# Two staging tiles, a separate mask matmul and a three-piece weight load in a recurrent attention kernel

## The chip, the cores and the metric

One core of a Trainium2 chip runs the whole program. The metric is the device time of one execution in microseconds (us). The kernel before took 2313.74 us (median of three runs, 2310.14 to 2330.06); its profiled execution took 2317.11 us, of which 2315.3 us lie between the first and the last instruction (the span).

## The reference

Two branches over the same input x (2048 rows of 1024, bf16) are mixed row by row with a gate. Branch B is a feed-forward net. Branch A is attention with a memory that is carried from segment to segment: 64 segments of 32 rows, each seeing 8 memory rows in front, 32 heads of 128.

```python
for s in range(n_seg):
    h = concatenate([mem, x[:, s*seg:(s+1)*seg, :]])     # 8 + 32 rows
    q, k, v = h @ Wq, h @ Wk, h @ Wv                     # 32 heads of 128 each
    p = softmax(where(mask, q @ k.T * scale, -1e9))
    o = (p @ v) @ Wo
    mem = o[:, :8]; outs.append(o[:, 8:])
a = concatenate(outs)
b = (gelu(x @ w_gate) * (x @ w_up)) @ w_down
g = sigmoid((x * gate_w).sum(-1)); out = g * a + (1 - g) * b
```

Segment s cannot start its projections before segment s-1 has given its 8 memory rows. The four attention weights are 32 MB in bf16 together, more than the core's on-chip memory holds.

## The kernel before

**Stages.** Up to about 1650 us of the span the program runs the 64 segments; after that come one pass over rows that were put aside and the feed-forward branch. The change touches the segments, and at the end of them two copies into `rb`.

**Rows of a segment.** TensorE takes 32 columns as its left side: 24 rows of the segment and the 8 memory rows (`hT0`, `hT1`, used in turn by segments). The other 8 rows of each segment need no memory for their own projections; they are projected four segments at a time from `hR` in the "fills" (`fill`, L844), and their results go out to the scratches `qk_scr` and `v_scr` and come back as `qkr` and `vB`.

**Heads and weights.** Heads come in two halves u = 0, 1. Each of Wq, Wk, Wv and Wo is cut into 8 pieces per half; a piece is 128 rows by 2048 columns, 512 KB or 4 KB per partition. Pieces with an index in `PAIRS` (two of k, two of q, five of v, five of o) share one slot between the two halves, so 14 of 64 pieces, 7 MB, are read again in every segment; the others stay. A slot is read again as soon as the last matmul on its old piece has run (`spent`). Some neighbouring slots are read by one DMA ("twins", `load_two`): k 0 and 1, q 0 and 1, v 0 and 1, v 2 and 3, o 4 and 5; v 4, o 0, o 1 and o 6 come alone. Wo is not laid out in the order that a piece needs, so a piece of it is written to `wo_scr` in segments 1 to 10 (`keep`) and from then on is read from there.

**Order.** All engines run lists in program order. The order comes from `walk` (the sequence of the 64 piece steps of a segment) and from hooks that `plan(s)` hangs on steps with `on(m, r, n, ...)`: m is the matrix, r = 0 the first half used in the segment and r = 1 the second, n the step. A segment's steps are: k r0 0-3, q r0 0-1, then o r1 4-7 of the segment before, q r0 2-3, v r0 0-3, k r0 4-7, q r0 4-7, v r0 4-7, then k r1, q r1, o r0, v r1 and o r1 0-3. `ua` and `ub` are the halves that a segment uses first and second. All weight loads, the load of the next `hT`, one load of `qkr` and the store of `oRc` are issued by SP, one after the other, and move through one DMA queue in that order; GpSimd (POOL) issues the loads of `vB` and of the other `qkr`, the stores of the fills and the store `a_scr` of a segment's output.

**One half of attention.** ACT copies k out of its PSUM bank into a staging tile (`evac`, L664), TensorE turns it (`turn`, L681), DVE copies it into `kT` (L667), POOL adds the 8 other rows from `qkr` (`put_rest`, L883); the same for q. `scores(u)` issues on TensorE the mask (one matmul of `mS` against the identity, 320 columns, L697) and 32 small score matmuls (L703) into bank SS, then the softmax on DVE and ACT up to `tAB` (L709 to L723). `attend(u)` (L732, L740) multiplies with `vA` and `vB`; `rest_o` (L757) puts 8 rows aside in `oRc`. After o r1, `fold` (L818, L819) adds two halves of the output through `part` into `a_bf`, and `next_mem` (L828, L831) turns the memory rows into the next `hT`.

**Who shares bytes with whom.** `hT0`, `vB` and `hT1` lie in a row, and `part` is two tiles over hT0+vB and vB+hT1. The staging tile of k of the second half ("p", `pS`) covers `oRc` and `a_bf`. The staging tile "o" covers `oT`, which is also `vA`: the second fill of a segment goes through it (`fill_evac`, `fill_put`, L876, store L879). Nearly every segment has a fill, two of four have a second one (`FILL`); the second is carried into the next segment.

Of the kernel before, what the change touches and what calls it, by code (L numbers as in the profile page):

```python
# [210 lines left out]
def bass_gated_mix__memory_aug_recurrent_mem_tr__geglu_ffn__prompt_kernel(  # L211
# [34 lines left out]
    with ExitStack() as es:  # L246
# [17 lines left out]
        wo_scr = nc.dram_tensor("wo_scr", [16, 128, 2048], BF16)  # L264

# [22 lines left out]
        hT0 = al("hT0", [128, KC, 32])  # L288
        vB = al("vB", [128, 2, 128])
        hT1 = al("hT1", [128, KC, 32])  # L290
        assert vB.off == hT0.off + 512 and hT1.off == vB.off + 512
        hT = (hT0, hT1)
        part = tuple(al(f"part{n}", [128, 256], FP32, at=o) for n, o in enumerate((hT0.off, vB.off)))
        qkr = al("qkr", [128, 3, 128])
        oRc = al("oRc", [128, NB, 32])
# [8 lines left out]
        assert a_bf.off == oRc.off + 512  # L304
        stage = {n: al(n + "S", [128, 512], at=t.off) for n, t in (("k", kT), ("q", qT), ("o", oT), ("p", oRc))}
# [69 lines left out]
        wo_at = lambda k: 8 * k[1] + k[2]  # L375

        def load_piece(t, k, lane):
            if k in kept:
                op("sp", lambda e: e.dma_start(t[:, :], wo_scr[wo_at(k)]), rd=[("D", "wo", k)], wr=[t.r()], lane=lane)
            else:  # L380
                op("sp", lambda e: e.dma_start(dst(t, k), src(k)), wr=[t.r()], lane=lane)

        def keep(k):
            t = slots[home[k]]
            op("sp", lambda e: e.dma_start(wo_scr[wo_at(k)], t[:, :]), rd=[t.r()], wr=[("D", "wo", k)], lane="wo")
            kept.add(k)
# [21 lines left out]
        twin = {("k", 1): 0, ("q", 1): 0, ("v", 1): 0, ("v", 3): 2, ("o", 5): 4}  # L408
        both = {}
        for (m, i1), i0 in twin.items():  # L410
            n0, n1 = home[m, 0, i0], home[m, 0, i1]
            assert i1 == i0 + 1 and n1 == n0 + 1 and slots[n1].off == slots[n0].off + PIECE
            both[m, i1] = ((wall, n0 - nkqv) if m == "o" else (sl, n0))
        held = set()

        def due(n):
            if done[n] < len(uses[n]) and uses[n][done[n]] != uses[n][done[n] - 1]:
                nk = uses[n][done[n]]
                return (nk, nk in moved and done[n] == len(uses[n]) - 1)
            return (None, False)  # L420

        def joined(k0, k1):
            return all(k is not None and not mv for k, mv in (k0, k1)) and (k0[0][0] != "o" or (k0[0] in kept and k1[0] in kept))

        def load_two(k0, t, x):
            m, u, i = k0
            k1 = (m, u, i + 1)
            reg = ("S", t.off + x * PIECE, t.off + (x + 2) * PIECE)
            if m == "o":
                a = wo_at(k0)  # L430
                op("sp", lambda e: e.dma_start(t[:, x:x + 2, :], wo_scr[a:a + 2].rearrange("y p c -> p y c")),
                   rd=[("D", "wo", k0), ("D", "wo", k1)], wr=[reg], lane=f"sl{home[k0]}")
            else:
                W = {"q": A_Wq, "k": A_Wk, "v": A_Wv}[m]
                v = W[i * 128:(i + 2) * 128, 16 * u:16 * u + 16, :].rearrange("(y p) h e -> p y (h e)", y=2)
                op("sp", lambda e: e.dma_start(t[:, x:x + 2, :], v), wr=[reg], lane=f"sl{home[k0]}")

        def reload(n, d):
            nk, mv = d
            if nk is None:  # L440
                return
            if mv:
                load_piece(moved[nk], nk, f"sl{n}")
            else:
                fetch(n)

        def spent(k):
            n = home[k]
            assert uses[n][done[n]] == k
            done[n] += 1  # L450
            m, u, i = k
            d = due(n)
            if (m, i + 1) in twin and d[0] is not None:
                held.add((m, i))
                both[m, i] = d
                return
            if (m, i) in twin and (m, i - 1) in held:
                held.remove((m, i - 1))
                d0 = both.pop((m, i - 1))
                if joined(d0, d):  # L460
                    load_two(d0[0], *both[m, i])
                    return
                reload(n - 1, d0)
            reload(n, d)
# [201 lines left out]
        def dve_copy(o, i, rd, wr):  # L666
            op("dve", lambda e: e.tensor_copy(o, i), rd=rd, wr=wr)  # L667
# [26 lines left out]
        def scores(u):  # L694

            def f(e):
                e.matmul(PB[SS][:, 0:320].rearrange("p (a c) -> p a c", a=4), lhsT=ident[:, :],  # L697
                         rhs=mS[:, :].unsqueeze(1).to_broadcast([128, 4, 80]), start=True, stop=False, skip_group_check=True)
                for n, c in ((32, 0), (8, 40)):
                    for j in range(4):  # L700
                        for g in range(4):
                            x = 8 * (4 * j + g)
                            ins = e.matmul(PB[SS][32 * g:32 * g + n, j * 80 + c:j * 80 + c + LQ],  # L703
                                           lhsT=qT[:, j, g, :] if n == 32 else qkr[:, 2 * u, x:x + 8],
                                           rhs=kT[:, j, g, :], start=False, stop=True, skip_group_check=True)
                return ins
            op("pe", f, rd=[qT.r(), qkr.r(256 * u, 256 * u + 128), kT.r(), ident.r(), mS.r()], wr=[BK(SS)])
# [14 lines left out]
            for c in (0, 256):  # L722
                op("dve", lambda e, c=c: e.transpose(tAB[:, c:c + 256], pAB[:, c:c + 256]), rd=[pAB.r(c, c + 256)], wr=[tAB.r(c, c + 256)], after=[fin])  # L723
# [91 lines left out]
        def fold(s, b):  # L815
            lo, hi = slice(64 * b, 64 * b + 64), slice(64 - 64 * b, 128 - 64 * b)
            pt, cs = part[s % 2], slice(256 * b, 256 * b + 256)
            op("dve", lambda e: e.tensor_copy(pt[lo, :], PB[XO][hi, cs]), rd=[BK(XO)], wr=[pt.r()])  # L818
            op("dve", lambda e: e.tensor_tensor(out=a_bf[lo, :], in0=PB[XO][lo, cs], in1=pt[lo, :], op=ALU.add),  # L819
# [83 lines left out]
        def plan(s):  # L903
# [29 lines left out]
            if not last:  # L933
# [10 lines left out]
            if s > 0:  # L944
                on("v", 0, 7, lambda: scores(ua))
# [3 lines left out]
            if s == 0:  # L949
                on("k", 1, 1, lambda: scores(ua))  # L950
# [7 lines left out]
            on(*(("q", 1, 1) if s else ("o", 0, 0)), lambda: evac(bank_of["k", 1], stage["p" if s else "k"], "act"))  # L958
            if s > 0:
                on("o", 0, 0, lambda: attend(ua, ((0, "dve"),), TT))  # L960
                on("o", 0, 0, lambda: evac(bank_of["q", 1], stage["q"], "act"))
                on("o", 0, 0, lambda: trans(kT, "p", A0))
                on("o", 0, 0, lambda: put_rest())
                on("o", 0, 0, lambda: take(((1, "act"), (2, "act"))))
                on("o", 0, 2, lambda: trans(qT, "q", SS))
# [3 lines left out]
            else:  # L969
# [4 lines left out]
                on("o", 0, 6, lambda: scores(ub))  # L974
# [38 lines left out]
        fold(NSEG - 1, 1)  # L1013
# [4 lines left out]
        for b in range(NBK):  # L1018
            rb = rbs[b % 2]
            for hf in range(2):  # L1020
# [9 lines left out]
                cp[("act", "dve")[hf]](rb[0:RB, hf * 512:hf * 512 + 512], PB[bk][0:RB, :], [BK(bk)], [rb.r(hf * 512, hf * 512 + 512)])  # L1030
# [143 lines left out]
```

## Time and profile before

| what | value |
|---|---|
| median of the runs shown (lowest to highest) | 2313.74 us (2310.14 to 2330.06) |
| profiled execution, and its span | 2317.11 us, 2315.3 us |
| TensorE matmul busy, weight load busy | 2130.5 us (92%), 1060.6 us (46%) |
| VectorE (DVE), ScalarE (ACT), GpSimd (POOL) busy | 1028.5 us, 543.2 us, 433.0 us |
| bytes moved by DMA | 638.35 MB |
| granted TensorE clock, mean | 0.986 |

In the lines of the profile, L774 is line 774 of the kernel before, and a tile name left of `<-` is what is written. "Idle before" is the time that the engine stood still ahead of an instruction, with what ended it. A timeline line gives start, duration, engine, line, operation and shapes; several instructions in a row are merged (x36). A DMA line is the issue, not the transfer; when a transfer has landed is read from its semaphore.

### The profile page before, as it was taken

The numbers are of one execution on the slowest core, as the hardware profiler recorded it, in microseconds if no ns is written. First come the engines' busy times: TensorE is split into PE (matmuls) and PEld (weight loads), VectorE is DVE, ScalarE is ACT, GpSimd is POOL, SyncE is SP. The second block draws the span as 40 slices with busy tenths as digits, with TensorE's granted clock in tenths as the row PEclk, the third lists the DMA queues.
The fourth block names the chain that finished last, engine by engine and source line by source line (L and its number), as shares of the span: only waits on it lengthen the run. The fifth ranks groups of instructions, "written<-read, shape, count | busy, mean of one in ns | idle before, by whom it ended". The sixth has DMA issues, their size and how long they took to land.

```text
span 2315.3 us, 74604 instructions
## 1 busy us (share of the span) xinstructions
PE 2130.5 (92%) x33852; PEld 1060.6 (46%) x33852; DVE 1028.5 (44%) x2440; ACT 543.2 (23%) x1111; POOL 433.0 (19%) x821
## 2 busy tenths in 40 slices
PE   4488999999999999999999999998899999999999
PEld 2244444444444444444454445444464444444444
DVE  3344444444444444444444444444315346163462
ACT  1122222222222222222222222222113123032130
POOL 4422222222222222222222222221100000000000
PEclk9799999999999999999999999999999999999999
DMA  9999999899898999989999899998964450803520
GB/s 373 353 306 333 333 338 348 305 337 333 314 336 319 328 340 324 345 323 334 347 327 349 310 335 345 320 331 319 340 201 159 137 163 10 285 25 117 178 88 19
DMA packets 251964, 638.35 MB, mean 276 GB/s; under 512 B 23256, under 2 KB 92120, under 8 KB 251648
## 3 DMA queue, kind: packets, MB, share of 16 engines
q1 hardware_dynamic: 227824, 596.59, 72.3%
q0 software_dynamic: 13888, 26.31, 3.8%
q10 hardware_dynamic: 9936, 10.69, 1.4%
q8 instruction: 266, 4.36, 0.7%
q14 instruction: 50, 0.41, 0.1%
HBM read 596.85 MB, written 36.63 MB: 274 GB/s over the span
## 4 chain that ended last, share of the span: by engine, by line
PE 66%; DMA 22%; DVE 4%; issue 4%; ACT 3%; POOL 1%; ACTq 0%; POOLq 0%; SPq 0%
PE pb L774 19%; PE pb L1075 15%; DMA sl<-in_A_Wv_dram 7%; PE pb L1129 5%; PE pb L807 5%; PE pb L844 5%; DMA qk_scr<-oS 4%; PE pb L790 4%; PE pb L681 3%; PE pb L1026 3%; PE pb L854 2%; DMA qkr<-qk_scr 2%; PE pb L1110 2%; DMA wall<-wo_scr 1%; DMA xr_scr<-xr 1%
## 5 line engine op out<-in xcount | busy, mean ns | idle before, releaser
L774 PE MATMUL pb<-sl,hT 128*32 128x512 bf16 x12288 | 771.9, 382 | 27.0 <-issue 19.4
L774 PEld LDWEIGHTS pb<-sl,hT 128*32 128x32 bf16 x12288 | 348.7, 97 | 310.5 <-issue 37.6
L844 PE MATMUL pb<-sl,hR 128*32 128x512 bf16 x3072 | 221.3, 390 | 2.4 <-issue 1.8
L1075 PE MATMUL pb<-xT,wg 128*128 128x512 bf16 x896 | 211.7, 379 | 0.7
L1075 PE MATMUL pb<-xT,wu 128*128 128x512 bf16 x896 | 211.7, 379 | 0.0
L807 PE MATMUL pb<-wall,oT 128*32 128x256 bf16 x4056 | 148.7, 274 | 17.8 <-DMA wall<-in_A_Wo_dram 7.0
L757 POOL COPY oRc<-oT 128x128 bf16<-128x128 bf16 x128 | 96.3, 752 | 361.7 <-DVE oT L667 360.2
L790 PE MATMUL pb<-wall,oT 128*32 128x512 bf16 x2048 | 153.2, 391 | 9.5 <-issue 6.2
L818 DVE COPY part<-pb 64x256 f32<-64x256 f32 x128 | 54.0, 422 | 235.3 <-PE pb L807 234.3
L664 ACT ACTIVATE kS<-pb 128x512 bf16<-128x512 f32 x127 | 75.8, 597 | 344.2 <-PE pb L774 322.4
L1129 PE MATMUL pb<-wd,GT 128*128 128x512 bf16 x672 | 146.3, 379 | 1.3 <-DMA wd<-in_B_w_down_dram 1.3
L711 ACT ACTIVATE E<-pb 128x320 bf16<-128x320 f32 x128 | 56.0, 438 | 371.6 <-DVE pb L710 371.6
L1083 ACT ACTIVATE s<-pb 128x512 f32<-128x512 f32 x112 | 66.8, 596 | 311.7 <-PE pb L1075 311.7
L1075 PEld LDWEIGHTS pb<-xT,wg 128*128 128x128 bf16 x896 | 87.2, 98 | 107.9 <-DVE GT L1091 3.7
L1075 PEld LDWEIGHTS pb<-xT,wu 128*128 128x128 bf16 x896 | 87.7, 98 | 105.7
L1084 DVE SCALAR_TENSOR_TENSOR tp<-s,pb 128x512 f32<-128x512 f32 x112 | 76.9, 687 | 124.2 <-ACT s L1083 124.0
L807 PEld LDWEIGHTS pb<-wall,oT 128*32 128x32 bf16 x4056 | 100.3, 96 | 67.6 <-ACT oT L664 26.1
L667 DVE CAST oT<-pb 128x160 bf16<-128x160 f32 x256 | 76.4, 320 | 115.2 <-PE pb L740 115.2
L667 DVE COPY kT<-pb 128x512 bf16<-128x512 bf16 x128 | 54.4, 425 | 158.1 <-PE pb L681 157.7
L664 ACT ACTIVATE vA<-pb 128x512 bf16<-128x512 f32 x128 | 76.2, 596 | 199.1 <-PE pb L774 151.7
L883 POOL COPY kT<-qkr 128x128 bf16<-128x128 bf16 x128 | 37.3, 292 | 431.2 <-DVE kT L667 272.5
L1088 DVE SCALAR_TENSOR_TENSOR tp<-tp,pb 128x512 f32<-128x512 f32 x112 | 77.0, 687 | 78.5 <-ACT tp L1087 78.5
(93 smaller groups left out, 2283.1 us busy)
## 6 DMA issues: line engine op xcount, KB each, us to landing
sl<-in_A_Wv_dram SPq DMA_DIRECT2D x128, 1024.0 KB, 11.2
wall<-wo_scr SPq DMA_DIRECT2D x175, 512.0 KB, 6.3
sl<-in_A_Wk_dram SPq DMA_DIRECT2D x64, 1024.0 KB, 5.8
sl<-in_A_Wq_dram SPq DMA_DIRECT2D x64, 1024.0 KB, 9.3
wall<-wo_scr SPq DMA_DIRECT2D x55, 1024.0 KB, 8.4
wd<-in_B_w_down_dram SPq DMA_DIRECT2D x42, 1024.0 KB, 5.6
sl<-in_A_Wv_dram SPq DMA_DIRECT2D x75, 512.0 KB, 11.6
wall<-in_A_Wo_dram SPq DMA_DIRECT2D x41, 512.0 KB, 7.7
```

The source lines that it names most:

```text
L664: op("act", lambda e: e.activation(o, i, ACTF.Copy), rd=rd, wr=wr)
L667: op("dve", lambda e: e.tensor_copy(o, i), rd=rd, wr=wr)
L681: ins = e.transpose(PBV[bank][:, j * 128:(j + 1) * 128], st[:, j * 128:(j + 1) * 128], ident[:, :])
L757: op("pool", lambda e: e.tensor_copy(oRc[:, :, 16 * u:16 * u + 16].rearrange("p c x -> p x c"), oT[:, :, :, 32:40].rearrange("p g j c -> p ...
L774: ins = e.matmul(PB[bk][32 * g:32 * g + 32, :], lhsT=h[:, i, :], rhs=w[:, g * 512:(g + 1) * 512], start=(n == 0), stop=(n == 7))
L790: ins = e.matmul(PB[XO][32 * g:32 * g + 32, :], lhsT=oT[:, j, x, 0:32], rhs=wall[:, na:nb + 1:nb - na, c:c + 256], start=(n == 0 and hp == 0),
L807: ins = e.matmul(PB[XO][32 * g:32 * g + 32, 256 * b:256 * b + 256], lhsT=oT[:, j, x, 0:32], rhs=w[:, c:c + 256], start=False, stop=(n % 4 ...
L844: ins = e.matmul(PB[b][32 * g:32 * g + 32, :], lhsT=h[:, k[2], :], rhs=w[:, g * 512:(g + 1) * 512], start=(n == 0), stop=(n == 7))
L1075: ins = e.matmul(PB[bk][:, 0:FB], lhsT=w[:, kc, cc:cc + 128], rhs=xT[:, :, :, kc, :].rearrange("p t i c -> p (t i) c"), start=(kc == 0), s ...
L1084: op("dve", lambda e, hg=hg, t=t: e.scalar_tensor_tensor(out=t[:, :], in0=s1[:, :], scalar=1.0, in1=hg, op0=ALU.add, op1=ALU.mult), rd=[BK ...
L1088: op("dve", lambda e, hu=hu, t=t: e.scalar_tensor_tensor(out=t[:, :], in0=t[:, :], scalar=1.0, in1=hu, op0=ALU.add, op1=ALU.mult), rd=[BK( ...
L1129: ins = e.matmul(PB[bank[2 * k + hf]][:, :], lhsT=GT[:, j, tb * 128:(tb + 1) * 128], rhs=w[:, jj, hf * 512:(hf + 1) * 512], start=(j == 0) ...
```

## The change

Line numbers of the new kernel differ by a few from those above; it keeps every computation.

1. Small tiles: the row is now `hT0`, `oRc`, `hT1`; `vB` has bytes of its own. The staging tiles 0 and 1 cover hT0+oRc and oRc+hT1 and replace "p" (k of the second half now goes through tile `ub`, the `hT` of the next segment) and "o" for the second fill (tile `ua`). `part` is one tile over `qT`. `a_bf` is no longer covered by a staging tile.
2. Moved because of that: the load of the next `hT` from k r0 4 to o r0 0, behind the turn of k; `load_v` of the next segment from q r0 2 to o r1 2 of the segment before; the copy out of the second fill's bank from q r0 2 to k r0 0, and its turn and store from v r0 3 to q r0 2.
3. The mask matmul is an operation of its own, right behind the turn of q (hooks v r0 5 and o r0 2); the second turn of q uses bank A1 in place of SS.
4. Pieces o 4, 5 and 6 lie in a scratch `wg_scr` as rows of 3 x 4 KB and are read by one DMA of 1.5 MB once all three slots are free.
5. Two copies at the end (`rb`) name the last `fold` as something to wait for.

```diff
+        wg_scr = nc.dram_tensor("wg_scr", [2, 128, 3, 2048], BF16)
...
         hT0 = al("hT0", [128, KC, 32])
+        oRc = al("oRc", [128, NB, 32])
+        hT1 = al("hT1", [128, KC, 32])
...
+        qkr = al("qkr", [128, 3, 128])
         vB = al("vB", [128, 2, 128])
-        part = tuple(al(f"part{n}", [128, 256], FP32, at=o) for n, o in enumerate((hT0.off, vB.off)))
...
+        part = al("part", [128, 256], FP32, at=qT.off)
+        stage = {n: al(f"{n}S", [128, 512], at=t.off) for n, t in (("k", kT), ("q", qT), ("o", oT), (0, hT0), (1, oRc))}
...
-        wo_at = lambda k: 8 * k[1] + k[2]
+        wo_at = lambda k: wg_scr[k[1], :, k[2] - 4, :] if 4 <= k[2] < 4 + 3 else wo_scr[8 * k[1] + k[2]]
...
+        GROUPS = {("k", 0): 2, ("q", 0): 2, ("v", 0): 2, ("v", 2): 2, ("o", 4): 3}
...
+                op("sp", lambda e: e.dma_start(t[:, x:x + n, :], wg_scr[u]), rd=[("D", "wo", (m, u, i + y)) for y in range(n)],
+                   wr=[reg], lane=f"sl{h}")
...
+        def mask():
+            op("pe", lambda e: e.matmul(PB[SS][:, 0:320].rearrange("p (a c) -> p a c", a=4), lhsT=ident[:, :],
+                                        rhs=mS[:, :].unsqueeze(1).to_broadcast([128, 4, 80]), start=True, stop=False,
+                                        skip_group_check=True), rd=[ident.r(), mS.r()], wr=[BK(SS)])
...
-            if not last:
+            if not last and s == 0:
                 on("k", 0, 4, lambda: load_h(s + 1))
...
             if s > 0:
+                on("v", 0, 5, mask)
                 on("v", 0, 7, lambda: scores(ua))
...
-            on(*(("q", 1, 1) if s else ("o", 0, 0)), lambda: evac(bank_of["k", 1], stage["p" if s else "k"], "act"))
+            on(*(("q", 1, 1) if s else ("o", 0, 0)), lambda: evac(bank_of["k", 1], stage[ub if s else "k"], "act"))
...
-                on("o", 0, 0, lambda: trans(kT, "p", A0))
+                on("o", 0, 0, lambda: trans(kT, ub, A0))
+                if not last:
+                    on("o", 0, 0, lambda: load_h(s + 1))
...
-                on("o", 0, 2, lambda: trans(qT, "q", SS))
+                on("o", 0, 2, lambda: trans(qT, "q", A1))
+                on("o", 0, 2, mask)
...
             if two:
-                on("q", 0, 2, lambda: fill_evac(*fl[1], B0, "o"), **nx)
+                on("k", 0, 0, lambda: fill_evac(*fl[1], B0, ua), **nx)
             on("q", 0, 2, lambda: fold(s, 1), **nx)
-            on("q", 0, 2, lambda: load_v(s + 1), **nx)
+            if two:
+                on("q", 0, 2, lambda: fill_put(*fl[1], ua, SS), **nx)
+            on("o", 1, 2, lambda: load_v(s + 1))
             on("v", 0, 3, lambda: next_mem(s, 1), **nx)
-            if two:
-                on("v", 0, 3, lambda: fill_put(*fl[1], "o", SS), **nx)
```

More of the change, by code (lines that the diff above doesn't have):

```diff
@@ L406, in first @@
                 fetch(n)
[L408 to L414, printed above, removed]
+        GROUPS = {("k", 0): 2, ("q", 0): 2, ("v", 0): 2, ("v", 2): 2, ("o", 4): 3}
+        lead = {(m, i + x): (m, i) for (m, i), n in GROUPS.items() for x in range(n)}
+        for (m, i), n in GROUPS.items():
+            assert all(home[m, 0, i + x] == home[m, 0, i] + x for x in range(n))
+        held = {}
         def due(n):
@@ L418, in due, with load_group, reload @@
                 nk = uses[n][done[n]]
[L419 to L425, printed above, removed]
+                return nk, nk in moved and done[n] == len(uses[n]) - 1
+            return None, False
+        def load_group(k0, n):
             m, u, i = k0
[L427 to L428 removed]
+            h = home[k0]
+            t, x = (wall, h - nkqv) if m == "o" else (sl, h)
+            reg = ("S", slots[h].off, slots[h].off + n * PIECE)
             if m == "o":
[L430 to L432 removed]
+                op("sp", lambda e: e.dma_start(t[:, x:x + n, :], wg_scr[u]), rd=[("D", "wo", (m, u, i + y)) for y in range(n)],
+                   wr=[reg], lane=f"sl{h}")
             else:
                 W = {"q": A_Wq, "k": A_Wk, "v": A_Wv}[m]
[L435 to L445, printed above, removed]
+                v = W[i * 128:(i + n) * 128, 16 * u:16 * u + 16, :].rearrange("(y p) h e -> p y (h e)", y=n)
+                op("sp", lambda e: e.dma_start(t[:, x:x + n, :], v), wr=[reg], lane=f"sl{h}")
+        def reload(n, nk, mv):
+            if nk is not None:
+                if mv:
+                    load_piece(moved[nk], nk, f"sl{n}")
+                else:
+                    fetch(n)
         def spent(k):
@@ L450, in spent @@
             done[n] += 1
[L451 to L455, printed above, removed]
-                return
[L457 to L464, printed above, removed]
+            g = lead.get((k[0], k[2]))
+            if g is None or due(n)[0] is None:
+                reload(n, *due(n))
+                return
+            q = held.setdefault(g, [])
+            q.append((n, *due(n)))
+            if len(q) == GROUPS[g]:
+                del held[g]
+                if any(mv for _, _, mv in q) or (k[0] == "o" and not all(nk in kept for _, nk, _ in q)):
+                    for x in q:
+                        reload(*x)
+                else:
+                    load_group(q[0][1], len(q))
         pw = lambda t, f, first=False: op("pool", f, rd=[] if first else [t.r()], wr=[t.r()])
@@ L692, in bass_gated_mix__memory_aug_recurrent_mem_tr__geglu_ffn__prompt_kernel, with scores @@
         b8 = lambda v, n: v.unsqueeze(2).to_broadcast([128, 8, n])
-        def scores(u):
+        def mask():
+            op("pe", lambda e: e.matmul(PB[SS][:, 0:320].rearrange("p (a c) -> p a c", a=4), lhsT=ident[:, :],
+                                        rhs=mS[:, :].unsqueeze(1).to_broadcast([128, 4, 80]), start=True, stop=False,
+                                        skip_group_check=True), rd=[ident.r(), mS.r()], wr=[BK(SS)])
+        def scores(u, masked=True):
+            if not masked:
+                mask()
             def f(e):
-                e.matmul(PB[SS][:, 0:320].rearrange("p (a c) -> p a c", a=4), lhsT=ident[:, :],
-                         rhs=mS[:, :].unsqueeze(1).to_broadcast([128, 4, 80]), start=True, stop=False, skip_group_check=True)
                 for n, c in ((32, 0), (8, 40)):
@@ L706, in f @@
                 return ins
-            op("pe", f, rd=[qT.r(), qkr.r(256 * u, 256 * u + 128), kT.r(), ident.r(), mS.r()], wr=[BK(SS)])
+            op("pe", f, rd=[qT.r(), qkr.r(256 * u, 256 * u + 128), kT.r()], wr=[BK(SS)])
             op("pool", lambda e: e.memset(pAB[:, 256:544].bitcast(FP32), 0.0), wr=[pAB.r(256)])
```

30 lines of the change are left out of this document (13 added, 17 removed).

## The prediction

> **What bounds the kernel now.** I read the page first.
>
> ```profile
> PE 2130.5 (92%) x33852; PEld 1060.6 (46%) x33852; DVE 1028.5 (44%) x2440; ACT 543.2 (23%) x1111; POOL 433.0 (19%) x821
> ...
> PE   4488999999999999999999999998899999999999
> ...
> DMA  9999999899898999989999899998964450803520
> ```
>
> In the segments (28 of 40 slices) TensorE and the DMA engines both look full. Matmul ends are modelled, so short stalls hide in that 9; I therefore went on to one segment. The windows of a single period, from one issue of the Wk load (920.12) to the next (943.65), show the DMA share beside the rest:
>
> ```profile
> 920.12:921.12 1.00, 1.00 (x32) 0.67 (x28) 0.00 (x0) 0.00 (x0) 0.00 (x0) 1.00 0.16 51
> 921.12:923.12 2.00, 2.00 (x53) 1.19 (x45) 0.88 (x3) 0.60 (x1) 0.09 (x1) 1.00 0.69 178
> 923.12:942.12 19.00, 18.12 (x388) 8.80 (x386) 10.23 (x28) 5.84 (x13) 6.10 (x13) 1.00 1.02 386
> 942.12:943.65 1.53, 1.53 (x31) 0.76 (x33) 0.17 (x1) 0.00 (x0) 0.95 (x2) 1.00 0.69 197
> ```
>
> The last two columns are DMA share and GB/s: for 19 of 23.5 us the queue is full, then it runs dry until Wk can be issued, which TensorE releases with k r0 1. So a period is a loop: Wk issued, then Wq, Wv and the last Wv piece landing in queue order, then the last v r1 matmul, attend, o r1, fold, the next memory, Wk again. I measured it in the 50 periods from 407 to 1618 us, from issues, landings and starts, always from the issue of Wk: period 24.21 us; last Wv piece landed at 17.57; last v r1 matmul began at 18.18; the tail from there is 6.04 (24.21 less 18.18). In 19 of 50 that matmul began within 0.05 us of the landing; in the others TensorE came later. So the segment time is the **later of two paths**, W (weights) and P (TensorE's way to v r1), plus the tail. The waits and timelines tell what delays P:
>
> ```profile
> POOL kT L883 <- DMA qkr<-qk_scr: 135.3, 25, 6.4
> ...
> ACT vA L664 <- DMA qk_scr<-oS: 47.4, 24, 2.9
> ```
>
> ```profile
> 926.14 0.40 PE L681 MATMUL pb<-ident,qS 128*128 128x128 bf16 x4
> 926.47 0.61 PE L774 MATMUL pb<-sl,hT 128*32 128x512 bf16 x8
> 927.05 0.31 PE L697 MATMUL pb<-mS,ident 128*128 128x320 bf16 x1
> 927.29 0.28 PE L703 MATMUL pb<-kT,qT 128*32 128x40 bf16 x16
> ```
>
> In the waits (total us, times, longest), vA: in the periods with a second fill (24 of 50), vA waits until the store of `oS`, which lies in the same bytes, has landed: vA begins 0.08 us after that landing in every one, at 11.2 against 8.85 elsewhere. The copy of k into `pS` begins 0.07 to 0.09 us after the landing of `a_scr<-a_bf` in nearly all of the 50 (mean 11.16): its bytes are a_bf's. kT: POOL adds `qkr` to kT 0.12 us after it has landed in 26 of 50 (mean landing 12.96). In the timeline the mask stands between qT's arrival and the scores and takes 0.24 us there (927.05 to 927.29), twice per segment.
>
> **The change part by part.**
>
> *Removed, on path P.* (1) The mask's 0.24 us, twice: it moves behind the turn of q, where TensorE waits for DVE's copy of q anyway (turn starts 926.14, mask 927.05, with 8 matmuls between, 0.44 us by the 3.72 that 68 of them take elsewhere in the chain). Without that cover it costs the same 0.24 as before. (2) vA no longer waits for the fill's store, pS no longer for a_scr. The earliest start of attend in the 50 was 10.98 us, the mean 11.60; so 10.98 - 0.24 = 10.74. What is late next is `qkr`. The earliest second mask was at 13.27; the scores would then start at 13.27 - 0.24 = 13.03, but qkr gives 12.96 + 0.12 + 0.29 (POOL's copy) + 0.08 = **13.45** on average. Before they started at 14.28 + 0.24 = 14.52. The last v r1 matmul follows 18.18 - 14.52 = 3.66 later, so P = 17.11.
>
> *Removed, on path W.* The load of hT (128 rows of 512 B) stood ahead of the last Wv piece and moves behind it; vB's load, of the same size, moves out of this stretch to the end of the period before. A 512 B packet takes 27 ns and each of 16 engines has 8: 0.22 us each. W = 17.57 - 0.44 = 17.13. Bounds: nothing, if the two fit gaps (share 0.69 at the start), and 0.44.
>
> *The two together.* Both means are now equal; the landings scatter by 0.34 (Wv) and 0.70 (qkr), the root of the squares' sum is 0.78, and the later of two such times is on average 0.4 x 0.78 = 0.31 behind either: 17.43. The waits that I count as code loading (TensorE's idle time put down to "issue", about 27 us in the 50 periods) stay; I leave 0.15 of their 0.54 per period uncovered. 17.58 against 18.18: **0.60 gained**.
>
> *Added.* (3) One DMA for o 4 to 6 is issued at o r0 5 instead of 3. Issue costs nothing: Wv still fills the queue then (6 was issued at 15.2 in the period shown, Wv lands at 17.8), and SP's lists stay in order; the moved hT load stands on SP ahead of Wo 0, which waits for a later matmul. But pieces 4 and 5 now land with 6, at 24.38 in place of some 1.3 us earlier, and are wanted at o r1 5, about 1.1 us after the next Wk issue: slack before 24.21 + 1.6 - 24.38 for piece 6, now 23.7 + 1.1 - 24.4 = 0.4. With a scatter of 0.6 the wait is 0.08 on average. (4) The second fill's copy now writes over oRc, so ACT waits for `o_scr<-oRc` (landing 24.88, after Wo); copy 0.60 and two handovers, so its turn can start at 25.66, 1.9 to 2.0 us after the new Wk issue, where TensorE arrives at 1.74 (there DVE's second fold usually begins). Behind it stand q r0 2 on TensorE and the hT copy on DVE: 0.2 in half the periods. It lies on P, which has 13.45 - 13.03 = 0.42 to spare. Its store, issued near 3.1 instead of 4.06, must have landed (7.0 us later) before k's copy, wanted at 11.2: free. (5) With an earlier tail o r1 3 needs Wo 1 at 20.1, about when it lands: 0.05. Price of 3 to 5: **0.12**.
>
> (6) Size of run: 12 KB is not in this trace. Nearest rows: 4096 B packets of the same queue, 159 ns median, 178 mean; 8192 B code packets, 307 at best; 16,384 B code packets, 1036. Per 12 KB that is 3 x 178 = 534, 460 or 777 ns; 8 per engine make -0.6 to +1.9 us per load. I take 0, by the same queue's rows. The final copies and `part` cost nothing (DVE idles 2.99 us before fold).
>
> *Sum.* 0.60 - 0.12 = 0.48 us x 62 periods = 30 us, from 2317.1 to 2287 in the profiled execution. The median lies 3.4 us under that execution: **2284**. 1% is 23 us, about what a measurement here can tell from no change.
>
> **The rivals.**
> - *A, W does not move* (0.20). The queue carries the same bytes, and the two small loads may have used gaps. Against it: share 1.02 for 19 us. The later of 17.57 and 17.11 averages 17.70; with the 0.15 and 0.12 the gain is 0.21: 2301.
> - *B, new waits in place of old* (0.14). Both Wo's three pieces and o_scr behind them end near the next period's start; if they come 0.5 us later than worked out (vB now moves then), half the gain goes: 2299.
> - *C, slow 12 KB runs* (0.13), the one on the other side. If they run like the 16,384 B packets, three pieces land at 26.3 while o r1 5 wants them at 24.8: TensorE stands 1.5 us, P = 13.03 + 1.5 + 3.66 = 18.2, W slips by half a us as the tail fills the queue's dry stretch, the later is 18.5: 0.3 to 0.5 lost in 54 periods, 2328 to 2340. It turns at about 1.5 us of extra landing. For it: the only packets over 8 KB in the trace are slow, in idle stretches too. Against: 8 KB at 307 ns. The Trainium skill (DMA: Bandwidth & Descriptors, SWDGE vs HWDGE vs iDMA) prefers packets of at most 4096 B, the unit after which an engine may change queues; no run here shows what a longer one does, and by that rule the small queues too would wait behind each run.
> - *D, more* (0.05): qkr also lands sooner without vB ahead of it: P drops another 0.4, 2262.
>
> **How the numbers follow.** Forecast 0.48, alone 2264 to 2298, of it 0.40 faster by over 1% and 0.08 within. A: 0.06 and 0.14. B: 0.12 within, 0.02 slower. C: 0.05 within, 0.08 slower. D: 0.05 faster. Faster 0.51, within 0.39, slower 0.10. The range 2256 to 2320 leaves out most of C and the edge of D.
>
> **What would show it.** Right: vA never waits for qk_scr; the copy of k into tile 0 or 1 starts near 10 us; second scores near 13.5, last Wv near 17.1, period 23.7. Wrong: packets of 12,288 B over 600 ns, or TensorE idle at o r1 5 or at the second fill's turn.

## The result, and the profile after

The changed kernel takes **2302.58 us** (median of 15 runs, 2291.61 to 2308.10) beside 2316.56 us of the kernel before (15 runs, 2310.01 to 2330.06): a ratio of 0.9935, 95% interval 0.9922 to 0.9949. That is 14 us, or 0.65%. Timed once more beside other kernels it was 0.9957 (0.9936 to 0.9979). The forecast was 2284, a gain of 30 us: the direction is right, but half of the gain is missing.

The profiled execution took 2308.1 us, its span 2306.3. The page of after, parts 1 and 2:

```profile
PE 2119.9 (92%) x33852; PEld 1048.7 (45%) x33852; DVE 1028.8 (45%) x2440; ACT 541.4 (23%) x1111; POOL 423.7 (18%) x821
...
PE   4598999999999999999999999998899999999999
...
DMA  9989999898998999999989899999964440903520
```

The page looks the same: 10.6 us less TensorE and the same two full rows. One period again says more. The windows of a period of after (columns: window, its length, busy time of PE, PEld, DVE, ACT and POOL, clock, DMA share, GB/s):

```profile
1104.08:1105.08 1.00, 1.00 (x32) 0.67 (x28) 0.00 (x0) 0.17 (x1) 0.00 (x0) 1.00 0.09 26
1105.08:1107.08 2.00, 2.00 (x52) 1.07 (x40) 1.19 (x3) 0.43 (x1) 0.00 (x0) 1.00 0.83 178
1107.08:1125.40 18.32, 17.28 (x388) 8.92 (x384) 9.64 (x28) 5.83 (x13) 5.22 (x11) 1.00 1.00 373
1125.40:1127.42 2.02, 1.90 (x36) 0.88 (x34) 0.46 (x2) 0.00 (x0) 1.91 (x4) 1.00 0.88 331
```

In the long third window the queue is full here as before (share 1.00 over 18.32 us, and 1.02 over 19.00; the edges are set by hand). One thing is new at the start: ACT works there in the first microsecond (0.17), before the fold. That is the second fill's copy, moved ahead. The waits of after (engine, line, what it waited for: us in total, times, longest):

```profile
POOL kT L880 <- DMA qkr<-qk_scr: 214.9, 40, 6.7
ACT vA L656 <- PE pb L771: 153.0, 65, 6.1
...
ACT 0S L656 <- DMA o_scr<-oRc: 50.5, 11, 5.2
ACT 1S L656 <- DMA o_scr<-oRc: 39.7, 9, 5.3
...
ACT 0S L656 <- DMA qk_scr<-0S: 11.0, 13, 1.6
...
ACT 1S L656 <- DMA qk_scr<-1S: 9.8, 13, 1.3
```

The old line "vA behind the store of oS" is gone, as is pS behind a_scr. In their place the second fill's copy waits for the store of `oRc` (in the 50 periods 23 of 24 of these copies begin 0.08 us after that landing), and `qkr` is what POOL waits for. The last two lines show a wait that I had called free: k of the second half goes through the same tiles, so its copy waits until the second fill's store has landed. In the three executions of after it begins 0.08 us behind that landing in 24, 23 and 24 of the 24 periods with a second fill, at 10.6 to 10.8 us, against 9.7 to 9.8 in the others.

I measured the 50 periods again (407 to 1618 us), from two profiled executions of before, three of after, and one of each variant below. A mean of 50 periods scatters by 0.15 us from its own spread alone, so these rows tell where time lies; verdicts go by the timed ratios. Mean us per stretch; "code" is TensorE's idle time put down to "issue", summed over the period:

| stretch of the period | before | after | mask alone | merged load alone | both of these | after, turn put back |
|---|---|---|---|---|---|---|
| Wk issue to first scores | 7.22 | 7.25 | 6.94 | 7.25 | 7.06 | 7.02 |
| to first attend | 4.43 | 4.21 | 4.63 | 4.35 | 4.62 | 4.24 |
| to second scores | 2.94 | 2.75 | 2.73 | 2.84 | 2.74 | 2.76 |
| to last v r1 matmul | 3.55 | 3.75 | 3.69 | 3.60 | 3.68 | 3.78 |
| tail | 6.04 | 6.14 | 6.08 | 6.04 | 5.92 | 6.09 |
| period | 24.17 | 24.10 | 24.07 | 24.08 | 24.01 | 23.89 |
| of it code | 0.63 | 0.87 | 0.65 | 0.54 | 0.66 | 0.76 |

The second and third stretch became 0.22 and 0.19 shorter, as meant. The third owes it to the mask: with the mask alone it is as short (2.73), and TensorE's idle time in it is 0.43 us before and 0.44 after. But the first, where the mask's 0.24 should be missing, did not shrink, and the fourth grew by 0.20.

### The profile page after: what moved, and what is told of

It reads as the page before. It is cut to its first block, busy times and chain, and to the rows that moved or that the text cites. A ratio compares the mean times of both kernels' runs of the same rounds, so it can differ in the third digit from the quotient of the medians.

```text
span 2306.3 us, 74586 instructions
## 1 busy us (share of the span) xinstructions
PE 2119.9 (92%) x33852; PEld 1048.7 (45%) x33852; DVE 1028.8 (45%) x2440; ACT 541.4 (23%) x1111; POOL 423.7 (18%) x821
## 4 chain that ended last, share of the span: by engine, by line
PE 70%; DMA 19%; issue 4%; DVE 4%; ACT 2%; POOL 1%; ACTq 0%; SPq 0%; POOLq 0%
PE pb L771 23%; PE pb L1077 15%; DMA sl<-in_A_Wv_dram 7%; PE pb L1131 5%; PE pb L841 5%; PE pb L804 4%; PE pb L787 4%; PE pb L673 3%; DMA qkr<-qk_scr 3%; PE pb L1027 3%; PE pb L1112 2%; PE pb L851 2%; DMA wall<-wg_scr 2%; DMA xr_scr<-xr 1%; DMA o_scr<-oRc 1%
## 5 line engine op out<-in xcount | busy, mean ns | idle before, releaser
L771 PE MATMUL pb<-sl,hT 128*32 128x512 bf16 x12288 | 778.4, 383 | 28.8 <-issue 16.9
L771 PEld LDWEIGHTS pb<-sl,hT 128*32 128x32 bf16 x12288 | 337.5, 97 | 331.6 <-issue 50.8
L841 PEld LDWEIGHTS pb<-sl,hR 128*32 128x32 bf16 x3072 | 82.3, 98 | 70.7 <-issue 20.8
## 6 DMA issues: line engine op xcount, KB each, us to landing
sl<-in_A_Wv_dram SPq DMA_DIRECT2D x128, 1024.0 KB, 10.8
```

The costliest lines, as they stand in the source:

```text
L771: ins = e.matmul(PB[bk][32 * g:32 * g + 32, :], lhsT=h[:, i, :], rhs=w[:, g * 512:(g + 1) * 512], start=(n == 0), stop=(n == 7))
L841: ins = e.matmul(PB[b][32 * g:32 * g + 32, :], lhsT=h[:, k[2], :], rhs=w[:, g * 512:(g + 1) * 512], start=(n == 0), stop=(n == 7))
```

## The experiments

**Two kernels again, and two things left out.** Before and after once more for the spread of profiles (2313.94 and 2311.24 us). Then after without the loads of Wv that the segments share; those pieces stay stale. And after without the warming matmuls.

```
 spent(k), after done[n] += 1:           (no Wv)
+    if k[0] == "v":
+        return
 plan(s):                                (no warming)
-    on("k", 0, 0, some(f2, 4) if two else lambda: warm(5), **nx)
+    on("k", 0, 0, some(f2, 4) if two else lambda: None, **nx)
     ...
-    on("k", 0, 0, some(f2, 4) if two else lambda: warm(2), **nx)
+    on("k", 0, 0, some(f2, 4) if two else lambda: None, **nx)
```

> The kernel before once more, for a second profile of it. The code theory says: the new kernel gained 0.7 us in every period in which TensorE does not wait for code (23.79 to 23.08 us in the first two profiles), and waits for code, which the slack ahead of the last Wv piece used to cover, give most of it back. It expects here about 0.7 us of waits for code per period, give or take 0.15, and again about 23.8 us in the periods without one. The rival that one profile of each misleads expects sums of such waits anywhere between 0.6 and 1.0, and periods without them that differ from 23.8 by over 0.3.

> The changed kernel once more. Code theory: 23.1 us (23.0 to 23.25) in periods without a wait for code, a mean period of 23.9 to 24.1, and 0.7 to 0.95 us of waits for code per period. Rival, the new waits (the three Wo pieces that land together, the turn of the second fill behind the store of oRc) take the gain: then periods without a wait for code are no shorter than 23.4.

> The changed kernel without the reloads of the shared Wv pieces in the segments (2.5 of 7 MB per period; v of the second half is then computed with the first half's weights). The weight path is gone and the queue is empty for some 6 us of a period. Code theory: waits for code come from the full queue, so they fall from 0.9 to under 0.4 us per period, and the period to 22.5 to 23.2 us, about 2240 to 2260 us in all. Rival, TensorE's waits put down to issue are its own and have nothing to do with the queue: they stay at 0.7 to 0.9 per period and the period stays above 23.4.

> The changed kernel without the 28 warming matmuls in the segments that have no second fill (56 fewer TensorE instructions in a half of the periods, 2.6% of the code of the segments; nothing reads what they compute). Code theory: fewer blocks of code to fetch (about 7 of 266), waits for code fall by some 0.05 us per period, and the time by 2 to 8 us, if the granted clock stays at 0.98. Rival, the clock: without them the granted clock falls and the kernel is slower than the changed one, by 10 us or more.

The second profiles leave it open whether code takes the gain. Before has 0.56 us of code per period and 23.6 us in the periods without such a wait, both within what the code theory expected. After has 0.83, as that theory expected, but 23.4 in the periods without, which is the rival's number; there are only 16 of them, with a standard error of 0.33. (The first execution of after had 23.1, the third 23.4.)

Without the Wv loads: 2224.75 us in a single run, and 2216.86 (2211.79 to 2218.77) when timed later, both below the 2240 to 2260 expected; the period is 22.95. The costliest row of TensorE on three pages, after, no Wv, no warming (busy us, mean ns | idle us before, and what ended it):

```profile
L771 PE MATMUL pb<-sl,hT 128*32 128x512 bf16 x12288 | 778.4, 383 | 28.8 <-issue 16.9
```

```profile
L773 PE MATMUL pb<-sl,hT 128*32 128x512 bf16 x12288 | 763.8, 382 | 6.6 <-issue 5.8
```

```profile
L771 PE MATMUL pb<-sl,hT 128*32 128x512 bf16 x12288 | 788.1, 388 | 35.4 <-DMA sl<-in_A_Wv_dram 12.7 <-issue 12.4 <-DVE hT L828 8.8
```

With 168 MB less in the queue the "issue" stalls of this row fall from 16.9 to 5.8 us, and from 0.87 to 0.16 us per period over all rows. What they are shows in the timeline of after (start, us, engine, line, operation, xcount, [idle before]):

```profile
1408.74 0.62 PE L841 MATMUL pb<-sl,hR 128*32 128x512 bf16 x8
1409.17 0.59 PE L771 MATMUL pb<-sl,hT 128*32 128x512 bf16 x5
1411.00 1.26 PE L771 MATMUL pb<-sl,hT 128*32 128x512 bf16 x20 [1.24 <-issue]
```

TensorE stops in the middle of a run of equal matmuls, with weights and hT there since long. Of the 51 such stalls over 150 ns between 400 and 1600 us, the middle 80% end 1.29 to 1.54 us after a 16,384 B packet of the instruction queue has ended; a random moment is 0.7 to 6.2 us behind one. Before has the same (46 stalls, 1.24 to 1.51). So the stalls go with the arrival of code, and there are fewer where the weights leave the DMA engines free. That TensorE waits for its own code, and the code behind the weights, is the reading that fits both; no run changes the loading of code alone. The Trainium skill (Runtime: NRT & Kernel Launch, Instruction fetch mechanics) says that each engine refills its instructions in 16 KiB blocks of 256 by a queue of its own, and calls the cost mostly hidden. The blocks fit (266 packets for some 68,000 instructions of TensorE), but here 0.6 to 0.9 us of a period of 24 are not hidden.

Without the warming matmuls: 2316.82 us, ratio 1.0008 (0.9985 to 1.0031), so all of the gain is lost: warming is worth about 14 us. TensorE issues 728 matmuls less in the 50 periods and code stalls stay at 0.85 us, so fewer instructions do not help here. The mean matmul of that row goes from 383 to 388 ns, and the mean granted clock of the profiled run from 0.983 to 0.974. But most of that fall has nothing to do with warming. The windows of the first 130 us, after and then no warming (the clock stands ahead of the last two columns):

```profile
0.00:130.00 130.00, 68.04 (x909) 33.60 (x910) 43.62 (x88) 21.55 (x39) 52.39 (x62) 0.82 0.96 350
```

```profile
0.00:130.00 130.00, 69.04 (x908) 32.83 (x908) 43.68 (x88) 21.55 (x39) 52.52 (x62) 0.71 0.96 350
```

The two kernels run the same matmuls in the same order up to 179 us, so this difference can't come from what was left out; it is about two thirds of the fall. In the 50 periods the clock is 0.990, against 0.996, 0.992 and 0.993 in the three executions of after. Worked out from these shares that is 2 to 7 us in these 1200, an estimate in which every bit of lost clock costs time. So the clock is at most a part of the 14 us, and the rest stays open: in this profile the last Wv lands at 17.52, as late as in before, and the stretch from second scores to v r1 takes 4.04 us.

**Each part undone.** After with the Wo scratch as before (pair and single, 4-KB rows); with the mask back; before with mask and merged load only (buffers undone); after with the three pieces in one DMA but from 4-KB rows.

```
-GROUPS = {..., ("o", 4): 3}             (no group)
+GROUPS = {..., ("o", 4): 2}
-wo_at = lambda k: wg_scr[k[1], :, k[2] - 4, :] if 4 <= k[2] < 4 + 3 else wo_scr[8 * k[1] + k[2]]
+wo_at = lambda k: wo_scr[8 * k[1] + k[2]]          (no group, and 4-KB rows)
-    e.dma_start(t[:, x:x + n, :], wg_scr[u])          (no group, and 4-KB rows)
+    e.dma_start(t[:, x:x + n, :], wo_scr[a:a + n].rearrange("y p c -> p y c"))
-    on("v", 0, 5, mask)                 (no mask)
-    on("v", 0, 7, lambda: scores(ua))
+    on("v", 0, 7, lambda: scores(ua, False))
-    on("o", 0, 2, lambda: trans(qT, "q", A1))
-    on("o", 0, 2, mask)
+    on("o", 0, 2, lambda: trans(qT, "q", SS))
-    on("o", 0, 4, lambda: scores(ub))
+    on("o", 0, 4, lambda: scores(ub, False))           (False: scores issues the mask itself)
```

> After with the scratch of Wo as it was: the three pieces in two DMAs (a pair and a single) of 4-KB rows. Theory 1 (the new order shortens the period by about 0.7 us, and stalls of TensorE for its own code, 0.8 to 0.9 us per period against 0.6 to 0.7 before, give half of it back): the merged load is worth nothing either way, 2298 to 2308 us, stalls still 0.8 to 0.9 us per period, periods without a stall 23.0 to 23.4 us. Rival 2 (the one wait for all three pieces and the larger block in the queue take the gain back): 2294 us or less, and the idle time behind Wo (2.3 us in the 50 periods) and the stalls fall to before's.

> After with the mask back in front of both scores and the second turn of q in its old bank; buffers and merged load stay. Theory 1: each scores group is 0.24 us longer again and the second one also waits for the bank, so 0.24 to 0.49 us per period, half of it taken from code stalls that then fall in the wait: 2310 to 2320 us. If the mask was hidden behind the landing of qkr and the code stalls anyway (rival 3): 2300 to 2306 us.

> Before with the mask and the merged load of after; the small buffers stay where they were. Theory 1: vA waits for the store again (14 us in 50 periods), pS for the landing of a_scr (4.6 us), and the last Wv lands 0.4 us later again: 0.2 to 0.4 us per period, 2310 to 2322 us. Rival 4 (the buffers moved waits without use, all of the gain is the mask): 2300 to 2306 us.

> After with the merged load of three pieces kept as one DMA, but from rows of 4 KB. Theory 1: packets of 12 KB took 478 ns, three of 4 KB 3 x 180 ns, which is 0.06 us of 16 engines per KB-row triple and 0.25 us per load of 1.5 MB at most; the load is at the queue's end of the period where nothing waits: 2300 to 2310 us, at most 8 us above after. If larger packets are what holds code and small transfers up (rival 5): 2294 us or less, with code stalls at 0.7 us per period or less.

| kernel | median us | ratio to before | 95% |
|---|---|---|---|
| no group | 2310.33 | 0.9964 | 0.9945 to 0.9984 |
| no mask | 2299.24 | 0.9912 | 0.9886 to 0.9939 |
| buffers undone | 2311.85 | 0.9969 | 0.9950 to 0.9988 |
| one DMA, 4-KB rows | 2304.96 | 0.9935 | 0.9910 to 0.9959 |

Taking the merged load out costs 0.3% against the first timing of after, above the 2298 to 2308 us of theory 1, which had it neutral. The intervals still touch, and against a second timing of after (below) it is 0.1%; that the load is a gain, where the forecast had a price, is shown by the run with it alone, further below. The length of the run is nothing: one DMA from 4-KB rows has the very ratio of after. In the trace of after a 12,288 B packet takes 478 ns on average (462 median, 6784 packets), three of 4096 B in before 3 x 178. Undoing the buffers costs 0.3% in the same way (0.1% against the second timing). And putting the mask back costs nothing at all; it fell below both of the times that I expected.

**The mask once more, and without Wv.**

> After once more, unchanged, on the same chip as the version with the mask put back: 2302 to 2306 us by both theories.

> After with the mask back in front of both scores, timed once more beside after. Theory 7 (the 0.24 us that the mask's move takes from the second scores comes back as a wait for code or for Wv between the scores and v r1): within 4 us of after. Rival 8 (the moved mask and the turn of q in another bank cost something themselves): faster than after by 4 us or more.

> Before without the reloads of Wv shared by the segments (the last pieces of Wv are stale, 168 MB less are read). With the queue lightened, the change without its loads took 2225 us and TensorE waited for code 0.16 us per period. Theory 1 (TensorE's own path became 0.4 to 0.7 us per period shorter by the change, and code stalls give it back where the queue is full): here both kernels are without code stalls, so this one is 25 to 43 us slower than the change without its loads: 2250 to 2268 us, 23.2 to 23.5 us per period. Rival 6 (the edits are worth only the 14 us that the timing shows, and code has nothing to do with it): 2235 to 2243 us.

> The change without the reloads of Wv once more, timed: 2225 us, 22.95 us per period, code stalls 0.2 us per period or less. It stands beside before without the same loads; both theories expect the same of it.

After: 2307.58 (0.9957, 0.9936 to 0.9979). With the mask back: 2298.83 (0.9929, 0.9914 to 0.9944). Rival 8 is met by the medians, 8.7 us, though the two intervals overlap; what is sure is that the mask's move brings nothing here. Before without Wv: 2231.89 us (0.9638, 0.9621 to 0.9656) against 2216.86 (0.9571, 0.9555 to 0.9587), 15 us apart. Before lies below both of its ranges, but the distance is the 14 us of rival 6 and not the 25 to 43 of theory 1. So the missing gain was not all eaten by code: code stalls are 0.13 and 0.15 us per period here. What is larger here than in before is TensorE's idle time ahead of the first scores, 0.47 against 0.07 us per period: 0.21 of it behind the three pieces of Wo and 0.15 behind the turn of 0S and 1S.

That sent me to the order of that stretch. The timelines of a period with a second fill, from before (its Wk issue is at 824.93):

```profile
825.57 1.05 PE L807 MATMUL pb<-wall,oT 128*32 128x256 bf16 x32
826.44 1.25 PE L774 MATMUL pb<-sl,hT 128*32 128x512 bf16 x20
827.63 0.23 PE L828 MATMUL pb<-ident,a_bf 64*128 64x64 bf16 x2
827.79 0.40 PE L681 MATMUL pb<-ident,oS 128*128 128x128 bf16 x4
828.12 2.13 PE L774 MATMUL pb<-sl,hT 128*32 128x512 bf16 x36
830.18 0.40 PE L681 MATMUL pb<-ident,kS 128*128 128x128 bf16 x4
```

and from after (Wk issue at 1104.08), with the weight loads of the fill's turn and of the next memory's turn:

```profile
1104.72 1.05 PE L804 MATMUL pb<-wall,oT 128*32 128x256 bf16 x32
1105.70 0.40 PE L673 MATMUL pb<-ident,0S 128*128 128x128 bf16 x4
1106.03 1.26 PE L771 MATMUL pb<-sl,hT 128*32 128x512 bf16 x20
1107.23 0.23 PE L825 MATMUL pb<-ident,a_bf 64*128 64x64 bf16 x2
...
1109.57 0.40 PE L673 MATMUL pb<-ident,kS 128*128 128x128 bf16 x4
```

```profile
1105.70 0.23 PEld L673 LDWEIGHTS pb<-ident,0S 128*128 128x128 bf16 x4 [0.21 <-ACT 0S L656]
...
1107.22 0.11 PEld L825 LDWEIGHTS pb<-ident,a_bf 64*128 64x128 bf16 x2 [0.42 <-DVE 0S L873]
```

In before the fill's turn stands behind the next memory's turn (a_bf), where TensorE would otherwise wait for DVE's copy of hT: there it is covered. In after it stands ahead of 20 matmuls and of a_bf's turn, which moves from 2.70 to 3.15 us after the Wk issue (medians), and DVE's 0.42 us copy of 0S stands ahead of that turn too. The four matmuls of the fill's turn take 0.33 us there, and their weight load waits 0.21 us for ACT, of which some 0.1 shows in the matmuls. The turn of k follows at 5.49 in place of 5.25. That is 0.24 us, and it is just what the mask saves: the first scores of these periods (medians of every fourth one, which has a second fill) begin at 7.17 in after and 7.18 in before, but at 6.94 with mask and merged load only.

**The turn put back, and the parts alone.**

```
-    if two:
-        on("q", 0, 2, lambda: fill_put(*fl[1], ua, SS), **nx)
     on("o", 1, 2, lambda: load_v(s + 1))
     on("v", 0, 3, lambda: next_mem(s, 1), **nx)
+    if two:
+        on("v", 0, 3, lambda: fill_put(*fl[1], ua, SS), **nx)
```

> After with the turn and the store of the second fill back behind the second next memory (v r0 3), its copy still early and in the bytes of hT or oRc. Theory 9 (in the 24 of 50 periods with a second fill the turn's four matmuls stand ahead of the first next memory's turn and push it from 2.70 to 3.15 us, and all behind it by 0.24 us or more, which is the mask's gain): first scores in these periods back from 7.4 to 7.1 us, TensorE's wait for 0S and 1S gone, 0.10 to 0.24 us per period in all, half of which code may take: 2293 to 2301 us. Rival 10 (code and the landing of qkr take back whatever comes early): 2302 to 2308 us, code stalls at 1.0 us per period.

> The same with the mask back in front of the scores, which measured 2299 us with the turn early. Theory 9: first scores in the periods with a second fill from 7.6 to 7.3 us, 3 to 8 us faster than that: 2291 to 2296 us. Rival 10: 2297 to 2301 us. If the turn was what cancelled the mask's gain, this one is no longer faster than the one with the mask moved.

> Before with the mask's move alone (and the second turn of q in the other bank). Mask and merged load together, without the buffers, gave 0.9969. Theory 11 (the mask's 0.24 us twice are hidden by the landing of qkr, by Wv and by code): 2312 to 2317 us. Rival 12 (they are worth most of the joint gain, the merged load nothing): 2305 to 2309 us.

> Before with the merged load of Wo alone. Taking it out of after cost 0.3%. Theory 11: it is worth about 7 us here too, 2305 to 2311 us, with shorter stalls in the tail. Rival 12: 2313 to 2318 us.

| kernel | median us | ratio to before | 95% |
|---|---|---|---|
| after, turn put back | 2297.20 | 0.9902 | 0.9886 to 0.9918 |
| the same, mask back too | 2296.11 | 0.9898 | 0.9881 to 0.9916 |
| before, mask's move alone | 2315.76 | 1.0001 | 0.9983 to 1.0019 |
| before, merged load alone | 2308.71 | 0.9958 | 0.9942 to 0.9974 |

Theory 9 holds where the mask is moved: 2297.20 us lies in its range. The timeline of the first kernel (Wk issue at 1097.23) has before's order back, and TensorE arrives as early as there:

```profile
1098.75 1.25 PE L771 MATMUL pb<-sl,hT 128*32 128x512 bf16 x20
1099.94 0.23 PE L825 MATMUL pb<-ident,a_bf 64*128 64x64 bf16 x2
1100.10 0.40 PE L673 MATMUL pb<-ident,0S 128*128 128x128 bf16 x4
...
1102.48 0.40 PE L673 MATMUL pb<-ident,kS 128*128 128x128 bf16 x4
```

First scores in the periods with a second fill are at 7.0 us (after: 7.3 to 7.5). The gain over before grows from 0.65% (0.43% in the second timing) to 0.98%: the early turn cost 0.3 to 0.6%, some 8 to 13 us, with the mask moved. With the mask back it cost less, 0.1 to 0.3% (0.9898 against 0.9912 and 0.9929), and there the intervals overlap, though the first scores come 0.4 us sooner. The kernel with the turn put back is about 23 us faster than before, of the 30 that were forecast. With the turn back, the mask's place makes no difference (0.9902 and 0.9898), so the move was not harmful by itself; alone it is worth 1.0001. The merged load alone is worth 0.42%. The late turn has a price too: the fill's store is issued at 4.09 us in place of 3.5, the copy of k behind its landing begins at 11.06, and TensorE stands 0.22 us for it in each period with a second fill, against 0.02 in after.

**What covers the mask.**

> Before with the mask's move alone, and without the reloads of Wv shared by the segments (stale pieces, as in the other runs without them). In the full kernel the mask's move was worth nothing (1.0001). Theory 13 (TensorE's path does become 0.24 us shorter at each scores, but the last Wv, qkr and code cover it; here Wv is gone, qkr lands 2 us earlier and code stalls are 0.13 us per period): 0.4 to 0.5 us per period faster than before without the loads (2231.9), 2202 to 2208 us. Rival 14 (the mask's matmul costs the path nothing even uncovered): 2228 to 2234 us.

> The change with the second fill's turn put back, without the reloads of Wv. With the turn early it took 2216.9 us, and TensorE waited 0.15 us per period for 0S and 1S. Theory 9: the turn's 0.24 us or more in 24 of 50 periods and these waits go, 0.25 to 0.4 us per period: 2192 to 2202 us. Rival 15 (the waits behind Wo's three pieces, 0.2 us per period here, and the copy behind o_scr bound it): 2212 to 2218 us.

Before's level on this chip was 2324.11 us against 2315.4 in the batch above, so I compare ratios: mask alone without Wv 0.9550 (0.9515 to 0.9585; 2217.03 us) against 0.9638, and the change with the turn back 0.9510 (0.9476 to 0.9544; 2208.73 us) against 0.9571. By the periods, 22.85 against 23.09 and 22.79 against 22.95. So where Wv and qkr do not cover it the mask's move gives 0.24 us per period, where the full kernel gives 0: half of what theory 13 expected. Of the other half, ahead of the first attend, 0.11 us goes to code and 0.08 to waits for pieces of Wo and Wq. In the stretch from first scores to first attend the code stalls double when TensorE comes 0.2 us sooner, from 0.08 to 0.15 us without Wv and from 0.08 to 0.15 in the full kernel. The second pair lies between theory 9 and rival 15: the waits for 0S and 1S are gone, but 0.26 us per period behind Wo's three pieces remain.

## Why the prediction was half right

- **Path W: right.** Forecast 17.13 for the last Wv landing; the three executions of after have 17.18, 17.10 and 17.22 (before 17.57 and 17.54). The two 64-KB loads did stand in the way, and rival A falls.
- **vA: right; pS: without effect.** vA never waits for a store, the copy of k not for a_scr: 0.25 and 0.10 us of TensorE's idle time per period went. In the first case 0.04 came back as code in the same stretch. In the second code took 0.04 and the copies of oT 0.05, so nothing was left of it.
- **The second fill's store: not free.** It was to land well before the copy of k. That copy waits for it in every period with a second fill (10.6 to 10.8 us against 9.8). That this costs TensorE only 0.02 us is owed to the early turn; with the turn late it is 0.22.
- **The runs of 12 KB: right** at nothing; rival C falls (478 ns, not over 600).
- **The merged load: wrong sign.** I priced its wait at 0.08 us per period, and the wait is there (0.066 ahead of the first scores). But the load is a gain: 0.42% alone, some 10 us; taken out of after, 0.1 to 0.3%, which is not clear of noise. With 4-KB rows the time is the same. Landings of Wo are about the same (24.26 to 24.47 in after, 24.38 and 24.44 in before), and the stretches of one profile each do not settle where the time is won.
- **Path P: wrong, and this is the step that failed.** It has two errors. First, the second fill's turn: I priced only its wait ("0.2 in half the periods") and let it vanish in "0.42 to spare". Its own four matmuls and the wait for ACT's copy, moved from a covered place to one ahead of the path, cost 0.24 us and up in 24 of 50 periods; in all it took 8 to 13 of the 16 us that are missing. (With the mask back it took 3 to 7, not clear of noise.) Second, the 0.42 did not exist: 13.03 was the *earliest* arrival of the 50 less the mask, set against the *mean* landing of qkr. The mean arrival lies 0.9 to 1.2 us above the earliest in after, and TensorE's mean idle time ahead of the second scores is 0.80 (code 0.37, qkr 0.13, then Wo, turns and handovers). Second scores were forecast at 13.45 and came at 14.10, 14.24 and 14.30, and with the turn put back still at 14.03; v r1 at 17.58 forecast, 17.92 to 18.04 measured.
- **Code: mis-sized.** I took 0.54 us per period, let it stay and left 0.15 uncovered. My 27 us in 50 periods agree with one row alone, the weight loads of L774 (26.5); all of TensorE's matmul rows of that execution sum to 0.70 us per period, and its second execution has 0.56. The stalls rose by 0.24 per period (0.63 to 0.87), most of it from the second scores to v r1 (0.15 to 0.29), where TensorE now comes sooner. But the two executions of before have 0.23 and 0.08 in that stretch. With the parts undone or the turn back they are 0.54 to 0.76, with one at 1.01, so this number is the softest here.
- **Rival B** (new waits in place of old, 2299) is nearest to the truth, but mostly by another mechanism than it named: not later landings of Wo and o_scr but the place of the turn. **Rival D falls**: qkr lands no sooner (13.03 to 13.16 us against 12.96).

The sizes in one line: the merged load alone 0.4%, the mask nothing, and the buffers with the loads that they let move 0.6% over the merged load alone (0.9902 against 0.9958), of which the early turn left 0 to 0.2% (0.9957 and 0.9935 against 0.9958).

## What to carry to other kernels

When a step is moved, price the step itself at its new place, what stands behind it on every engine, and not only its wait: a 0.4 us turn that was free in a gap cost 0.3 to 0.6% at the head of the chain in the kernel as changed. Don't set an engine's earliest arrival against a mean landing; here they lay 0.9 to 1.2 us apart, small waits ahead of that point sum to 0.8, and a saving in front of such waits can be taken up by the next of them. And time the parts alone: of three edits one was worth nothing, and the one that I had down as a cost is worth 0.4% alone.

## What the runs showed of the hardware that I had not expected

- TensorE stood 0.6 to 0.9 us per period of 24 us, on average, with no releaser in the trace, where the DMA share averaged 0.91 to 0.93; 27 to 37 of 50 periods had such a stall. Where the share was near 0.7 it was 0.13 to 0.25 us. The middle 80% of the stalls ended 1.24 to 1.54 us after a 16,384 B instruction packet.
- Packets of 12,288 B ran at 478 ns, 25.7 B per ns, no worse than three of 4096 B at 178 ns each.
- Matmuls without a use, in a stretch where TensorE waits, were worth about 14 us (1.0008 against 0.9935); the granted clock of the 50 periods, 0.990 against 0.992 to 0.996, explains at most half of it.
- Two kernels that run the same matmuls in the first 130 us had a granted clock of 0.82 and 0.71 there, and two executions of before had 0.86 and 0.80, so a run's mean clock (0.983, 0.974) can't be put down to an edit without its place in time.
